# Attention with linear weights into a SwiGLU layer on one core: the first batch's loads, the order of the first weights, and the fourth batch's loads

## The chip, the cores and the metric

The kernel runs on one core of one Trainium2 chip. The metric is the device time of one execution in microseconds (us). A core has five engines that run side by side, each with its own queue of instructions that it takes in order: PE (TensorE, matmuls; its weight loads, PEld, overlap them), DVE (VectorE), ACT (ScalarE), POOL (GpSimd) and SP (SyncE, here for transfers alone). Transfers are issued from the queues of SP, ACT and POOL and run on 16 DMA engines that all of them share. An instruction waits for semaphores of others; what stands behind it on its engine waits with it.

## The reference

Eight batches of eight heads, 576 positions of 64 features. With `c`, `s` the cosine and sine of `pi/2 * pos/576`, every row of q and k becomes `[relu(x)*c, relu(x)*s]` (128 features). Attention is linear: K'V first, then Q' times that, over a denominator.

```
kv  = einsum('bhsf,bhsd->bhfd', k_p, v);  z = sum(k_p, axis=2)
num = einsum('bhsf,bhfd->bhsd', q_p, kv)
den = einsum('bhsf,bhf->bhs', q_p, z)[..., None] + 1e-06
x   = (num / den), heads side by side, reshaped to (4608, 512)
xn  = x / sqrt(mean(x*x) + 1e-6) * rms_g
out = (silu(xn @ w_gate) * (xn @ w_val)) @ w_out      # 512 -> 1536 -> 512
```

## The kernel before

**Tiles of the attention.** A batch's 576 positions are spread over 128 partitions: a pair of partitions shares 9 positions, 4 for one and 5 for the other (lines 83 to 87), so a batch is four tiles of 128 positions, j or t = 0 to 3, and a fifth that is half full (J). For this reason each load (`load`, line 92) is two DMAs, one for the even and one for the odd partitions, with 4 or 5 positions (1024 or 1280 B of float32) in a row; `cuts` splits the positions, so that a part can arrive earlier, in shorter rows. In the first batch k comes whole, q in positions 0 to 1 and 2 to 4, and v likewise, all issued from SP (lines 120 to 126). Batches 1 and 2 are loaded from POOL; from batch 3 on k and q come from ACT and v from POOL. v lands as bf16 from batch 1 on, which only POOL's transfers can do; the weights too.

**Steps of a tile.** `k_feat`, `q_feat` (lines 235, 247) make one half (cosine or sine, c = 0 or 1) of a feature tile on DVE or ACT; `v_cast` (238) copies v beside a column of ones. `kv_mm` (262) adds eight matmuls of tile j to K'V of all heads, in a PSUM tile of two banks (`att_tile`, two buffers), and `kv_evict` (275) copies it to SBUF on ACT. A q tile is turned either by a DMA from SP (`q_turn`, 281) or by eight PE transposes and a copy (`q_turn_pe`, `q_evict`, 290 to 305; PSUM from `ps_gv`, three buffers that the gate and value matmuls use as well). `num_mm` (309) makes numerator and denominator, `divide` (335, DVE) the quotient, `sumsq` (353) the sum of squares on ACT and its power -1/2, `rs`, on POOL, `norm` (364, DVE) the normed row; `x_turn_pe` and `x_evict` (380 to 392), or a DMA, turn it into columns of a block.

**Blocks of the feed-forward.** Nine blocks of 512 rows (the ninth is made of the half tiles J) run through `step(blk, nn)`, nn = 0 to 11 (line 626): gate matmuls to `gps`, value matmuls to `vps`, ACT's silu (`sil`), DVE's product `hT`, and from block 2 on four of the 48 output matmuls of the block before (`out_mm`, 438), which after each twelfth has ACT copy the result (`osb`) and SP store it (two DMAs). The first blocks take their columns in parts (`PARTS`), so that they can begin with fewer tiles. The 48 output matmuls of block 0 run in `lead()` (663), ahead of block 1, and fill the gaps of batch 1's preparation there.

**The order around it.** Everything is kept in the order of the program. Inside `step` the attention work of later batches is placed by a list: `at(g, kind, f, ...)` puts a call into step g (counted over all blocks) at one of the kinds `sp, act0, dve0, mid, act1, dve1, pe`, which `step` runs at fixed places:

```
run(g, "sp"); run(g, "act0"); run(g, "dve0")
gps matmuls; run(g, "mid"); vps matmuls
sil; run(g, "act1"); run(g, "dve1"); hT; out_mm x4 (from block 2 on); run(g, "pe")
```

**Weights.** `load_gv(c)` (209) issues two DMAs from POOL, a third of gate and of value weights; `load_wo(c)` a third of the output weights. Before, POOL first copies one element of the first cast v tile (`pool_after`, line 738), which holds its queue until then; thirds 0 and 1 follow, third 2 after `x_evict((0, 0))` (line 761), and at step 3 `more_loads` (152) issues the output weights and batches 1 and 2. At most eight of POOL's transfers are under way: each waits until the eighth before it has landed.

**Block 0's start** (lines 722 to 763) is written out: 34 warm-up matmuls on a tile of ones, features of k and of two q tiles, two turned q tiles, v casts with `kv_mm`, `num_mm`, and so on until the first normed tile is in place.

## Time and profile before

| what | value |
|---|---|
| median of 3 runs (lowest, highest) | 336.58 us (336.23, 337.99) |
| the profiled execution | 337.09 us, span on the core 334.9 us |
| busy in the span: PE, PEld | 318.3 us (95%), 213.4 us (64%) |
| busy in the span: DVE, ACT, POOL | 190.2 us (57%), 169.2 us (51%), 47.9 us (14%) |
| mean granted TensorE clock | 0.999 |
| moved by DMA | 50.63 MB, mean 151 GB/s |

The profile is of one execution. Its page lists busy times, forty slices, the DMA queues, the chain of waits that ended last, and groups of instructions; the trace behind it answers for single stretches: the timeline (start, duration, engine, line, operation; in square brackets the engine's idle time before it and what ended that), the waits by engine, the table by stretches (busy time of each engine, the granted clock, the share of the 16 DMA engines and GB/s, counted as written), and the DMA queues (q1 is issued by SP, q10 by ACT, q0 by POOL). A line such as L414 is a line of the kernel; L414 and L401 are gate and value matmuls, L446 output matmuls, L718 warm-up matmuls, L267 K'V, L316 the numerators, L294 and L384 the transposes on PE. A busy PE counts warm-up matmuls too, so its share says nothing of useful work at the start.

Some marks of the start, from the timeline and the transfers' times to landing (us from the span's start):

| event | us |
|---|---|
| k landed (two halves) | 5.3 and 7.2 |
| first q_turn_pe | 10.51 |
| first weight DMA issued | 12.51 |
| v's last cut landed, gb landed, q's last cut landed | 12.9, 13.6, 15.5 |
| kv_evict, first num_mm | 14.66, 15.30 |
| first gps matmul, first vps matmul | 20.30, 22.06 |
| lead() begins on PE | 44.1 |
| block 1, step 12, begins on PE | 60.1 |

### The profile page before, as it was taken

The numbers are of one execution on the slowest core, as the hardware profiler recorded it, in microseconds if no ns is written. First come the engines' busy times: TensorE is split into PE (matmuls) and PEld (weight loads), VectorE is DVE, ScalarE is ACT, GpSimd is POOL, SyncE is SP. The second block draws the span as 40 slices with busy tenths as digits, with TensorE's granted clock in tenths as the row PEclk, the third lists the DMA queues.
The fourth block names the chain that finished last, engine by engine and source line by source line (L and its number), as shares of the span: only waits on it lengthen the run. The fifth ranks groups of instructions, "written<-read, shape, count | busy, mean of one in ns | idle before, by whom it ended". The sixth has DMA issues, their size and how long they took to land.

```text
span 334.9 us, 7537 instructions
## 1 busy us (share of the span) xinstructions
PE 318.3 (95%) x3009; PEld 213.4 (64%) x3045; DVE 190.2 (57%) x394; ACT 169.2 (51%) x320; POOL 47.9 (14%) x91
## 2 busy tenths in 40 slices
PE   6679999998999999999999999999999999999995
PEld 4568856996887788778877744454444444444443
DVE  5676476776866575588857686665652422222300
ACT  3764377775875447486646474644433322233221
POOL 3446361300012120031103001000100000000000
PEclk9999999999999999999999999999999999999999
DMA  7999999893239989999969994253123021000012
GB/s 219 273 205 184 229 296 348 228 234 95 65 96 197 239 202 169 283 272 202 167 120 237 291 165 110 65 142 80 47 65 94 32 65 46 34 33 31 31 63 96
DMA packets 82147, 50.63 MB, mean 151 GB/s; under 512 B 49056, under 2 KB 76464, under 8 KB 82112
## 3 DMA queue, kind: packets, MB, share of 16 engines
q1 hardware_dynamic: 58032, 24.65, 33.8%
q0 software_dynamic: 13360, 13.57, 22.7%
q10 hardware_dynamic: 10720, 11.93, 12.2%
q8 instruction: 24, 0.39, 0.5%
q14 instruction: 11, 0.09, 0.1%
HBM read 38.01 MB, written 9.44 MB: 142 GB/s over the span
## 4 chain that ended last, share of the span: by engine, by line
PE 80%; DMA 7%; DVE 5%; ACT 4%; issue 2%; ACTq 1%; POOL 1%; SPq 0%; DVEq 0%
PE acc L446 25%; PE gps L401 12%; PE vps L401 12%; PE gps L414 12%; PE vps L414 12%; DMA rqT<-qp 3%; PE att L316 3%; DMA wv<-in_moe_w_val_dram 3%; PE att L267 2%; DMA kbuf<-in_k_dram 2%; DVE kp L231 1%; ACT kp L229 1%; PE qtp L294 1%; DVE xn L366 1%; PE acc L781 1%
## 5 line engine op out<-in xcount | busy, mean ns | idle before, releaser
L653 DVE TENSOR_TENSOR hT<-vps,sil 128x512 bf16<-128x512 f32 x108 | 74.5, 690 | 98.9 <-PE vps L401 59.6
L647 ACT ACTIVATE sil<-gps 128x512 bf16<-128x512 f32 x108 | 64.5, 597 | 109.6 <-PE gps L401 61.9
L446 PE MATMUL acc<-wo,hT 128*128 128x512 bf16 x395 | 101.8, 379 | 1.9 <-ACT osb L452 0.6
L446 PEld LDWEIGHTS <-hT 128*128 128x128 bf16 x420 | 40.0, 98 | 40.5 <-issue 0.9
L414 PE MATMUL gps<-xnT,wg 128*128 128x128 bf16 (+1 forms) x704 | 62.7, 239 | 0.7 <-ACT xnT L392 0.7
L414 PE MATMUL vps<-xnT,wv 128*128 128x128 bf16 (+1 forms) x704 | 62.8, 239 | 0.5 <-DMA wv<-in_moe_w_val_dram 0.5
L414 PEld LDWEIGHTS <-wg 128*128 128x128 bf16 x704 | 50.2, 98 | 6.8 <-DMA wg<-in_moe_w_gate_dram 0.6
L414 PEld LDWEIGHTS <-wv 128*128 128x128 bf16 x704 | 51.3, 98 | 3.8 <-DMA wv<-in_moe_w_val_dram 0.7
L361 POOL TENSOR_TENSOR rs<-ss,mhalf 128x1 f32<-128x1 f32 x36 | 20.1, 559 | 200.1 <-ACT sq L356 200.0
L401 PE MATMUL gps<-xnT,wg 128*128 128x512 bf16 x139 | 36.7, 379 | 0.4
L401 PE MATMUL vps<-xnT,wv 128*128 128x512 bf16 x141 | 36.5, 379 | 0.1
L452 ACT COPY osb<-acc 128x512 f32<-128x512 f32 x35 | 20.4, 583 | 26.4 <-PE acc L446 21.8
L401 PEld LDWEIGHTS <-wv 128*128 128x128 bf16 x192 | 18.8, 98 | 22.7
L366 DVE SCALAR_TENSOR_TENSOR xn<-x,rs,gb 128x512 bf16<-128x512 f32 x36 | 26.9, 748 | 8.8 <-POOL rs L361 8.8
L401 PEld LDWEIGHTS <-wg 128*128 128x128 bf16 x192 | 18.0, 98 | 20.1
L345 DVE TENSOR_TENSOR x<-att,rec 128x512 f32<-128x512 f32 x36 | 24.9, 691 | 1.2
L231 DVE TENSOR_SCALAR kp<-kbuf,trig 128x512 bf16<-128x512 f32 x50 | 22.8, 489 | 3.1 <-DMA kbuf<-in_k_dram 2.7
L231 DVE TENSOR_SCALAR qp<-qbuf,trig 128x512 bf16<-128x512 f32 x52 | 23.9, 485 | 0.4 <-DMA qbuf<-in_q_dram 0.4
L356 ACT ACTIVATE sq<-x 128x513 f32<-128x513 f32 x36 | 22.6, 626 | 2.9 <-DVE x L345 2.5
L229 ACT ACTIVATE kp<-kbuf,trig 128x512 bf16<-128x512 f32 x30 | 20.6, 712 | 3.4 <-DMA kbuf<-in_k_dram 3.4
L316 PEld LDWEIGHTS <-rqT 128*128 128x128 bf16 x320 | 14.3, 98 | 9.1 <-issue 1.1
L229 ACT ACTIVATE qp<-qbuf,trig 128x512 bf16<-128x512 f32 x28 | 19.6, 714 | 0.4 <-DMA qbuf<-in_q_dram 0.4
(63 smaller groups left out, 193.2 us busy)
## 6 DMA issues: line engine op xcount, KB each, us to landing
out_dram<-osb SPq DMA_DIRECT2D x70, 128.0 KB, 2.6
kbuf<-in_k_dram ACTq DMA_DIRECT2D x5, 640.0 KB, 6.1
qbuf<-in_q_dram ACTq DMA_DIRECT2D x5, 640.0 KB, 8.2
kbuf<-in_k_dram ACTq DMA_DIRECT2D x5, 512.0 KB, 4.8
qbuf<-in_q_dram ACTq DMA_DIRECT2D x5, 512.0 KB, 6.5
vbuf<-in_v_dram POOLq DMA_DIRECT2D x7, 320.0 KB, 9.4
vbuf<-in_v_dram POOLq DMA_DIRECT2D x7, 256.0 KB, 6.7
wg<-in_moe_w_gate_dram POOLq DMA_DIRECT2D x3, 512.0 KB, 10.1
```

Of the source, the lines that this page charges most:

```text
L229: K(nc.scalar.activation(out=dst, in_=src, func=AF.Relu, scale=scale))
L231: K(nc.vector.tensor_scalar(out=dst, in0=src, scalar1=scale, scalar2=0.0, op0=ALU.mult, op1=ALU.max,))
L316: K(nc.tensor.matmul(nums[key][:, h // Z, (h % Z) * E : (h % Z) * E + D + 1], lhsT=rqT[a, t][:, h, :], rhs=kvm[a % NK][:, h, 0 : D + 1], s ...
L345: K(nc.vector.tensor_tensor(out=x[:, 0:DM].rearrange("p (z s d) -> p z s d", z=2, d=D), in0=a[:, :, :, 0:D], in1=r.unsqueeze(3).to_broadca ...
L356: K(nc.scalar.activation(out=sq[:, :], in_=xs[key][:, :], func=AF.Square, scale=1.0 / math.sqrt(DM), accum_out=ss[:, :],))
L366: K(nc.vector.scalar_tensor_tensor(out=xn[:, :], in0=xs.pop(key)[:, 0:DM], scalar=rss.pop(key)[:, :], in1=gb[:, :], op0=ALU.mult, op1=ALU. ...
L401: K(nc.tensor.matmul(ps[:, :], lhsT=w[:, dt, nn * P : (nn + 1) * P], rhs=xnT[blk][:, dt, :], start=(dt == 0), stop=(dt == NDT - 1),))
L414: K(nc.tensor.matmul(ps[:, i * cn : (i + 1) * cn], lhsT=w[:, dt, (n0 + i) * P : (n0 + i + 1) * P], rhs=xnT[blk][:, dt, c0 : c0 + cn], star ...
L446: K(nc.tensor.matmul(acc[blk][:, :], lhsT=hT[blk][:, nn, jt * P : (jt + 1) * P], rhs=wo[:, nn, :], start=(nn == 0), stop=(nn == NNT - 1),))
L452: K(nc.scalar.copy(out=osb[:, :], in_=acc[blk][:, :]))
L647: K(nc.scalar.activation(out=sil[:, :], in_=gp[:, :], func=AF.Silu))
L653: K(nc.vector.tensor_tensor(out=dst, in0=a, in1=c, op=ALU.mult))
```

## The change

- **First batch's loads.** v comes in whole rows (no cuts). Of k the half with five positions is issued by ACT, and behind it, from ACT too, the weights of the norm (`gb`), which is now ahead of q; the rest stays on SP: half of k, q 0 to 1, v, q 2 to 4.
- **Features.** The first q tile's halves are made before the last k half of DVE (2, 1) and of ACT (4, 1).
- **Weights.** POOL's gate is now the first half of the first q tile (DVE); behind it all six gate and value DMAs and two of the three output weights are issued in one row. The third follows at step 0, with batch 1's k; q and v of batch 1 at step 2, batch 2 at step 3.
- **First K'V.** All v casts are placed ahead of the matmuls, tiles 1 and 3 on ACT; the order of tiles is 0, 1, 2, 4, 3; five warm-up matmuls go. K'V lies in two tiles of one bank each, from `ps_gv`, and ACT copies the first, DVE the second.
- **First normed tile.** `x_evict((0, 0))` is DVE's; `norm((0, 1))` stands before `divide((0, 2))`.
- **Kinds.** A kind `act2` behind `act1` takes ACT's features, casts and loads; in each third step from block 2 on it runs after the output matmuls. `q_turn` moves from `dve1` to `pe`.
- **Batch 1 and 2 in block 1.** q tile J of batch 1 goes from step 13 to 12, the first q tile of batch 2 from 14 to 13.
- **Fourth batch (b = 3).** k and v are issued in `lead()`, ahead of block 1, q at step 15, all from POOL.

```diff
@@ -89,14 +89,15 @@
 
 
 
+
     def load(t, src, b, odd_five=False, cuts=(0, NC5)):
-        if b == 0:
-            eng = nc.sync
-        else:
-            eng = nc.scalar if b > 2 and src is not v else nc.gpsimd
         for lo, hi in zip(cuts[:-1], cuts[1:]):
             for par, t0, jn in lanes(odd_five):
                 z = min(hi, jn)
+                if b == 0:
+                    eng = nc.scalar if src is k and jn == NC5 else nc.sync
+                else:
+                    eng = nc.scalar if b > 3 and src is not v else nc.gpsimd
                 K(eng.dma_start(
                     out=t[par:P:2, :, lo * D : z * D],
                     in_=src[b, :, :, :].rearrange("h (i j) d -> i h (j d)", j=NT)[
@@ -118,11 +119,11 @@
     clear_fifth(v0, nc.vector)
     gb = consts.tile([P, DM], FP32, name="gb")
     load_k(0)
-    load_q(0, (0, 2))
-    load_v(0, (0, 2, NC5))
-    K(nc.sync.dma_start(
+    K(nc.scalar.dma_start(
         out=gb[:, :], in_=moe_rms_g.rearrange("(o d) -> o d", o=1).to_broadcast([P, DM])
     ))
+    load_q(0, (0, 2))
+    load_v(0)
     load_q(0, (2, NC5))
 
 
@@ -259,13 +260,22 @@
     def att_heads(a):
         return a[:, :, 0 : Z * E].rearrange("p z (s w) -> p z s w", w=E)
 
+    def kv_banks(b):
+
+        t = kvp[b]
+        return t if b == 0 else [t[:, z, :] for z in range(2)]
+
     def kv_mm(b, j, first, last):
         if first:
-            kvp[b] = att_tile()
+            kvp[b] = (
+                [ps_gv.tile([P, TB], FP32, name="kv0", tag="gv") for _ in range(2)]
+                if b == 0 else att_tile()
+            )
+        banks = kv_banks(b)
         for h in range(H):
 
             K(nc.tensor.matmul(
-                kvp[b][:, h // Z, (h % Z) * E : (h % Z) * E + D + 1],
+                banks[h // Z][:, (h % Z) * E : (h % Z) * E + D + 1],
                 lhsT=kp[j][:, h, :, :].rearrange("p c d -> p (c d)"),
                 rhs=vx[j][:, h, 0 : D + 1],
                 start=(first and h % Z == 0),
@@ -274,9 +284,17 @@
 
     def kv_evict(b):
         dst = kvm[b % NK][:, :, :].rearrange("p (z s) w -> p z s w", z=2)
-        K(nc.scalar.copy(
-            out=dst[:, :, :, 0 : D + 1], in_=att_heads(kvp.pop(b))[:, :, :, 0 : D + 1]
-        ))
+        if b == 0:
+            for z, t in enumerate(kvp.pop(b)):
+                src = t[:, 0 : Z * E].rearrange("p (s w) -> p s w", w=E)[:, :, 0 : D + 1]
+                if z == 0:
+                    K(nc.scalar.copy(out=dst[:, z, :, 0 : D + 1], in_=src))
+                else:
+                    K(nc.vector.tensor_copy(out=dst[:, z, :, 0 : D + 1], in_=src))
+        else:
+            K(nc.scalar.copy(
+                out=dst[:, :, :, 0 : D + 1], in_=att_heads(kvp.pop(b))[:, :, :, 0 : D + 1]
+            ))
 
     def q_turn(b, t):
         tt = rqtp.tile([P, H, P], BF16, name="rqT", tag="rqT")
@@ -453,7 +471,7 @@
             out_store(blk, jt, osb)
 
 
-    KINDS = ("sp", "act0", "dve0", "mid", "act1", "dve1", "pe")
+    KINDS = ("sp", "act0", "dve0", "mid", "act1", "act2", "dve1", "pe")
     NS = (B + 1) * NNT
     plan = {(g, w): [] for g in range(NS) for w in KINDS}
 
@@ -475,18 +493,18 @@
     def feat_at(g, f, b, j, act):
         for c in range(2):
             on_act = c == 1 and act
-            at(g, "act1" if on_act else "dve0" if f == k_feat else "dve1", f, b, j, c, on_act)
+            at(g, "act2" if on_act else "dve0" if f == k_feat else "dve1", f, b, j, c, on_act)
 
     def q_at(g, b, t, act=False):
         feat_at(g, q_feat, b, t, act)
         if t < J:
-            at(g, "dve1", q_turn, b, t)
+            at(g, "pe", q_turn, b, t)
 
     def k_at(g, b, j, act=False):
         feat_at(g, k_feat, b, j, act)
 
     def v_at(g, b, j):
-        at(g, "act1", v_cast, b, j, True)
+        at(g, "act2", v_cast, b, j, True)
 
     def kv_at(g, b):
         for j in range(NC5):
@@ -513,18 +531,12 @@
         at(3, "dve1", q_feat, 0, J, c)
 
 
-    def more_loads():
-        for c in range(NG):
-            load_wo(c)
-        load_k(1)
-        load_q(1, (0, 2))
-        load_v(1)
-        load_q(1, (2, NC5))
-        load_k(2)
-        load_q(2)
-        load_v(2)
-
-    at(3, "pe", more_loads)
+    at(0, "pe", load_wo, 2)
+    at(0, "pe", load_k, 1)
+    for f, *a in ((load_q, 1, (0, 2)), (load_v, 1), (load_q, 1, (2, NC5))):
+        at(2, "pe", f, *a)
+    for f in (load_k, load_q, load_v):
+        at(3, "pe", f, 2)
 
     def pe_tile_at(g, key, xblk, col, gx):
 
@@ -537,9 +549,9 @@
 
     def q2_at(g, b, t):
         for c in range(2):
-            at(g, "act1" if c else "dve1", q_feat, b, t, c, c == 1)
+            at(g, "act2" if c else "dve1", q_feat, b, t, c, c == 1)
         if t < J:
-            at(g, "dve1", q_turn, b, t)
+            at(g, "pe", q_turn, b, t)
 
 
     at(12, "dve0", divide, (1, 2))
@@ -551,28 +563,27 @@
         at(12 + t, "dve0", norm, (1, t))
         at(12 + t, "pe", x_turn_pe, (1, t))
         at(13 + t, "act1", x_evict, (1, t), 1, t)
-    q2_at(13, 1, J)
+    q2_at(12, 1, J)
 
 
     for g, j, c in ((14, 2, 1), (15, 1, 0), (16, 0, 0), (16, 2, 0), (17, 3, 0), (17, 4, 0),
                     (17, 3, 1), (17, 4, 1)):
-        at(g, "act1" if c else "dve1", k_feat, 2, j, c, c == 1)
+        at(g, "act2" if c else "dve1", k_feat, 2, j, c, c == 1)
     for j in range(NC5):
-        at(18, "act1" if j > 2 else "dve1", v_cast, 2, j, j > 2)
+        at(18, "act2" if j > 2 else "dve1", v_cast, 2, j, j > 2)
     kv_at(18, 2)
-    for t, g in enumerate((14, 19, 20, 21, 23)):
+    pe_tile_at(19, (2, 0), 2, 0, 21)
+    for t, g in enumerate((13, 19, 20, 21, 23)):
         q2_at(g, 2, t)
-    pe_tile_at(19, (2, 0), 2, 0, 21)
     pe_tile_at(22, (2, 1), 2, 1, 24)
     pe_tile_at(24, (2, 2), 2, 2, 26)
     pe_tile_at(25, (2, 3), 2, 3, 27)
 
 
-    for o, f in ((12, load_k), (13, load_v), (15, load_q)):
-        at(o, "act1", f, 3)
+    at(15, "pe", load_q, 3)
     for j in range(NC5):
         for c in range(2):
-            at(22 + j, "act1" if c else "dve1", k_feat, 3, j, c, c == 1)
+            at(22 + j, "act2" if c else "dve1", k_feat, 3, j, c, c == 1)
         at(22 + j, "dve1", v_cast, 3, j)
     kv_at(27, 3)
     for t, g in enumerate((24, 25, 27, 28, 29)):
@@ -591,7 +602,7 @@
             (g1, g1 + 2, g1 + 4, g1 + 6),
         ))
         for o, f in zip(loads, (load_k, load_v, load_q)):
-            at(o, "act1", f, b)
+            at(o, "act2", f, b)
         for j, o in enumerate(preps):
             k_at(o, b, j, j > 1)
             v_at(o, b, j)
@@ -646,6 +657,9 @@
         sil = silp.tile([P, TB], BF16, name="sil", tag="sil")
         K(nc.scalar.activation(out=sil[:, :], in_=gp[:, :], func=AF.Silu))
         run(g, "act1")
+        ends = blk > 1 and nn % 3 == 2
+        if not ends:
+            run(g, "act2")
         run(g, "dve1")
         a, c = vp[:, :], sil[:, :]
         if blk in PARTS:
@@ -654,6 +668,8 @@
         if blk > 1:
             for i in range(4 * nn, 4 * nn + 4):
                 out_mm(blk - 1, i)
+        if ends:
+            run(g, "act2")
         run(g, "pe")
 
     def outs(lo, hi):
@@ -698,6 +714,8 @@
         norm((1, 0))
         outs(36, 40)
         q_turn_pe(1, 3)
+        load_k(3)
+        load_v(3)
         x_turn_pe((1, 0))
         x_evict((1, 0), 1, 0, dve=True)
         q_evict(1, 3)
@@ -722,24 +740,25 @@
     warm_up(34)
     for j in range(NC5):
         for c in range(2):
+            if (j, c) in ((2, 1), (NC5 - 1, 1)):
+                q_feat(0, 0, int(j > 2), act=(j > 2))
             k_feat(0, j, c, act=(j > 2))
-    for t in range(2):
-        for c in range(2):
-            q_feat(0, t, c, act=(c == 1))
+    for c in range(2):
+        q_feat(0, 1, c, act=(c == 1))
+    pool_after(qps[0, 0][0:1, 0, 0, 0:1])
+    for c in range(NG):
+        load_gv(c)
+    for c in range(2):
+        load_wo(c)
     q_turn_pe(0, 0)
     q_evict(0, 0, dve=True)
     q_turn_pe(0, 1)
     q_evict(0, 1)
     warm_up(8)
     for j in range(NC5):
-        v_cast(0, j, act=(j == 3))
-        kv_mm(0, j, j == 0, j == NC5 - 1)
-        if j == 0:
-            pool_after(vx[0][0:1, 0, 0:1])
-            load_gv(0)
-            load_gv(1)
-        if j == 1:
-            warm_up(5)
+        v_cast(0, j, act=(j % 2 == 1))
+    for j in (0, 1, 2, 4, 3):
+        kv_mm(0, j, j == 0, j == 3)
     kv_evict(0)
     num_mm((0, 0))
     num_mm((0, 1))
@@ -757,10 +776,9 @@
     num_mm((0, 2))
     q_feat(0, 3, 0, act=True)
     x_turn_pe((0, 0))
-    x_evict((0, 0), 0, 0)
-    load_gv(2)
+    x_evict((0, 0), 0, 0, dve=True)
+    norm((0, 1))
     divide((0, 2))
-    norm((0, 1))
 
 
     for blk in range(B + 1):
```

## The prediction

> **What bounds it now.** I read the busy shares first: PE is busy 95% of the 334.9 us span, DVE 57%, ACT 51%. So only time in which PE stands still can be won. The list of PE's waits says where that is.
>
> ```profile
> PE qtp L294 <- ACT qp L229: 2.6, 2, 2.1
> PE xps L384 <- DVE xn L366: 1.3, 3, 0.7
> PE att L316 <- DMA rqT<-qp: 0.8, 1, 0.8
> ...
> PE vps L414 <- DMA wv<-in_moe_w_val_dram: 0.5, 1, 0.5
> ```
>
> Next the table by stretches: in 0 to 22 us PE is idle 7.8 us (and its warm-up matmuls count as busy), afterwards only here:
>
> ```profile
> 44.00:60.00 16.00, 15.14 (x150) 8.75 (x151) 11.63 (x27) 12.39 (x22) 5.26 (x8) 1.00 1.16 310
> ...
> 72.00:88.00 16.00, 14.47 (x187) 12.83 (x187) 10.93 (x26) 11.53 (x23) 1.11 (x2) 1.00 0.52 120
> ```
>
> The second figure is the stretch, the third PE's busy time: 0.86 and 1.53 us are lost. In 30 to 44 us PE is busy 14.00 of 14.00. Third, the chain of waits, which for the start reads:
>
> ```profile
> 1.56 5.61 DMA kbuf<-in_k_dram
> ...
> 12.26 0.31 POOL probe L223
> 12.57 0.85 POOL wg L211
> 13.42 8.60 DMA wv<-in_moe_w_val_dram
> 22.02 0.05 issue
> 22.06 1.07 PE vps L414 x16
> ```
>
> k lands at 7.2; the weights wait for the first cast of v at 12.2, and wv's first third lands at 22.0, where PE needs it. But a second chain is as late: v's last cut lands at 12.9, kv_evict ends at 15.25, num_mm starts at 15.30, and through divide, sumsq, rs, norm, x_turn_pe and ACT's x_evict the first gps starts at 20.30 (timeline). Both must move. Last, PE's timeline around the two late stalls:
>
> ```profile
> 77.42 0.43 PE L316 MATMUL att<-kvm,rqT 128*128 128x65 bf16 x8 [0.80 <-DMA rqT<-qp]
> ...
> 82.06 0.40 PE L384 MATMUL xps<-ident_b,xn 128*128 128x128 bf16 x4 [0.72 <-DVE xn L366]
> ```
>
> **The start, DMA side.** v in whole lanes has rows of 1024 and 1280 B instead of 512 and 768 B. While k (rows of those sizes) flows, 4 to 6 us, the core moves 394 GB/s; while v's small rows flow, 8 to 10 us, 291. v's 1.18 MB by landings takes 3.9 us (three cuts 0.9 apart and 1.2 for the last); at 394 it is 3.0: -0.9. gb moves ahead of q: its 0.7 us (v's last landing 12.9, gb's 13.6) now lies before q and v: +0.7. v's last landing: 12.9 - 0.9 + 0.7 = 12.7, and all of q, k, v, gb ends 0.9 earlier.
>
> k over two queues: its 640 KB half leaves SP (0.73 us of issue) and is issued by ACT at 1.45 (after kbuf's memset) or, if the table load holds ACT's queue, at 2.02; no row here tells. Either way it now shares the engines with q instead of going ahead of it: half of q's 512 B rows, some 0.5 us, can come first. I take k at 7.7 (7.0 to 8.0) and q's first cut at 8.9 + 0.7 = 9.6.
>
> **The start, engines.** Started one behind the other, k's features take 0.62 us each on ACT (four in 2.56) and 0.41 on DVE (six in 2.47). ACT now runs three of them, 7.8 to 9.65, then the q feature to 10.3; so q_turn_pe(0, 0) starts at 10.4 (10.51 before). The gate is DVE's first q feature: five k features at 0.41 and q end at 10.3, probe 0.3, first weight issue at 10.6 against 12.51. The rest waits for v: casts on DVE to 13.95; on ACT, behind q_evict(0, 1), to 14.4; the last kv_mm (0.25 for eight) to 14.7 against 14.62. The five warm-up matmuls taken out filled that same wait and cost nothing. The eviction in two tiles: the last copies have 128x256 at 0.37 on ACT and 0.42 on DVE against 0.59 for the whole: num_mm at 15.2, -0.1. x_evict(0, 0) on DVE, 0.42 for 0.58: -0.16. First gps: 20.05.
>
> POOL now issues eight weight DMAs in one row, and rs(0, 0) queues behind them, wanted at 17.6. The rows run from 0.69 (DVE quiet) to 0.91 (DVE casting); eight are 5.5 to 7.3 us, so POOL is free between 16.1 and 17.9: 0 to +0.3. I take 0.8, done at 17.0: nothing. The Trainium skill, "SBUF — State Buffer", section "SBUF: two separate sides", speaks against the row of issues: while DVE runs some copies, GpSimd is locked out and cannot write descriptors. By that rule DVE's some 2 us of casts from 10.6 on would be added to 5.5: free at 18.1, +0.5; the 0.91 beside casts agrees in sign, not in that size.
>
> wv's first third no longer decides: the plain loads end 0.9 earlier, and the slow start of the weights' stream (some 80 GB/s between 14.5 and 15.5 against 206 later, worth 0.6 us) now lies beside them; 22.0 - 0.9 - 0.6 = 20.5, and vps wants it at 21.2 (gps 0.9 and x_turn_pe 0.25 later). So the first vps goes from 22.06 to 21.2. Much is given back: norm((0, 1)) now stands before divide((0, 2)) on DVE. DVE: x_evict to 20.0, norm to 20.75, divide 1.1, q feature 0.5, x_evict 0.4; sumsq and rs (1.4 after divide) let norm((0, 2)) end at 24.05, and its x_turn_pe holds the second vps at 24.35 against 24.69. **Start: -0.3.** Bounds: -1.3 (k not late, DVE's order free) and +1.7 (first rival).
>
> **The lead.** The nine weight DMAs and k(1) now follow without the break that the profile has at 30 to 32 us (119 GB/s instead of 206). k(1), landed at 44.9, comes some 2 us earlier. ACT, free from 44.0, waited 0.98 for it; its four k features, osb copy and q feature then end before PE asks at 48.1, and DVE's q feature (to 48.2) remains: PE's 0.56 there becomes some 0.1. **-0.5** (0 to -0.86, the stretch's whole idle).
>
> **Steps 12 to 22.** k and q of batch 3 leave ACT's queue: 1.6 us of issue between sumsq and sil at 61.55 to 63.2, and 1.2 at 67. q_feat(2, 0) moves from step 14 to 13 and q_feat(1, J) to 12; DVE's 0.72 of idle before hT at 62.12 covers the latter. rqT(2, 0) is then issued near 65 less what was won, before q(3) (now step 15, POOL). At 67.03 it was issued with q(3) and v(3) and took 10.34 us; the median transpose takes 3.9. Even at 10 us it lands before 76.6, when PE asks: -0.8. In step 20 sumsq now precedes the q feature (act2), 0.61 less in the chain to the late xps: -0.65. **-1.45** (0 to -1.7). If k(3) on POOL were slow, nothing waits: its features are due at 84, it is issued near 57, behind rs(1, 0) and rs(1, 1).
>
> **The rest.** q_turn now queues on SP behind a step's out_store: up to one step (2.6 us) later; num_mm comes three steps later, and 3.9 us of transpose fit. ACT's features behind osb in each third step may save PE's 0.6 of waits for osb: **-0.1** (+0.6 to -0.6).
>
> **Sum.** -0.3 - 0.5 - 1.45 - 0.1 = -2.35. The profiled execution took 337.09 us, 2.2 of it around its span; 334.7 for it. The median shown, 336.58, is 0.5 lower: 334.2.
>
> **Rivals.**
>
> *The rest of q is late.* q's last two cuts (1024 rows) are sent last, when the weights' packets now flow. If the rings alternate, some 560 rows left at 12.6 pair with weight packets (201 per us, 80 ns of 16 engines, against 34): 4.0 us, landing 17.6 instead of 15.5. sumsq((0, 0)) stands behind these q features on ACT: +1.7 at the start, 336.2. The rule is in "DMA: Bandwidth & Descriptors" of the Trainium skill, section "Queues, rings and completion order": each engine goes round its rings by packet. Against it is the stretch 14.5 to 15.0, when both had packets: what was in the ring first went first, 88 rows to 39.
>
> ```profile
> q0 software_dynamic: 39, 0.04, 113.9%
> q1 hardware_dynamic: 88, 0.06, 39.6%
> ```
>
> *The rest of q is starved: slower.* In 67 to 70 us it was the other way:
>
> ```profile
> q0 software_dynamic: 779, 0.42, 110.6%
> q10 hardware_dynamic: 138, 0.16, 14.4%
> ```
>
> v(3) had the engines, and the q DMA issued there took 9.4 us. If two of the weights' DMAs (2.55 us each) go in front of q's rest, it lands near 19.8, start +4: 338.5; with all eight 354. It is slower by over 0.5% if q's rest lands after 19.5.
>
> *The transpose's wait is only moved* (another transfer or DVE at step 21): the -1.45 falls away, 335.7. For it: DVE is 80% busy in 60 to 72.
>
> *The start gives nothing back* (k early, DVE's order harmless): -1.3, 333.2. For it, PE waits 2.1 us on ACT's q there; against it, v's landing.
>
> **How the numbers follow.** Forecast 0.45 (333.2 to 335.4); q's rest late 0.18; starved 0.10; wait moved 0.12; start in full 0.15. 0.5%, about what can be told from no change, is 1.7 us: faster is below 334.9. From the forecast some 0.38, all of the last 0.15 and 0.05 from the others: 0.58 faster; slower 0.12 (the starved case and unknowns); 0.30 between. The range runs from 332.3 to 336.8 and leaves out mostly the starved case.
>
> **What would show it.** Right: wv landed before the first vps; first gps near 20; no wait for rqT or 0.1 at the (2, 0) tiles; ACT's idle before the k(1) features gone. Wrong: ACT idle before the q features of tile 2 until after 16 us; rs(0, 0) behind weight issues; qtp later than 10.5; a new PE wait in 88 to 200.

## The result, and the profile after

The changed kernel is slower. Its median is 339.44 us (20 runs, 336.57 to 350.03) against 336.74 (20 runs, 336.18 to 340.21) for the kernel before on the same chip; the ratio of the compared runs is 1.0054, with an interval of 1.0028 to 1.008. The ratio leaves out runs more than 1.5% above a kernel's fastest, of which some of the kernels below have many, so the tables give the median of all runs, as its difference to the kernel before that ran beside it (here +2.70 us; the median before lies between 336.14 and 336.74 everywhere), and this ratio with its 95% interval next to it.

The profiled execution took 340.75 us, its span 338.6 (before 337.09 and 334.9). Line numbers moved: gate and value matmuls are now L432 and L419, output matmuls L464, warm-up L736, K'V and numerators L277 and L334, the transposes on PE L312 and L402, `q_turn` L301. PE's waits (total, times, longest):

```profile
PE qtp L312 <- ACT qp L230: 4.4, 2, 3.8
...
PE att L334 <- DMA rqT<-qp: 2.7, 1, 2.7
PE xps L402 <- DVE xn L384: 1.0, 3, 0.4
```

The wait for ACT's first q features grew from 2.6 to 4.4 us, one of 2.7 us for a turned q tile is new (the 0.8 us before were at another tile, near 77), and the wait for xn fell. The table by stretches (stretch, length, busy time of PE, PEld, DVE, ACT, POOL; granted clock, DMA share, GB/s):

```profile
12.00:22.00 10.00, 7.88 (x110) 6.42 (x111) 6.21 (x15) 6.88 (x13) 7.63 (x11) 0.83 1.20 233
22.00:30.00 8.00, 7.49 (x107) 7.26 (x105) 5.39 (x13) 2.72 (x5) 2.78 (x5) 0.79 1.24 206
...
44.00:60.00 16.00, 15.86 (x159) 10.38 (x159) 10.84 (x26) 11.20 (x20) 4.42 (x7) 1.00 1.03 280
...
72.00:88.00 16.00, 15.61 (x213) 14.27 (x211) 11.22 (x27) 11.93 (x22) 0.56 (x1) 1.00 0.39 109
150.00:160.00 10.00, 7.21 (x103) 5.78 (x103) 6.48 (x15) 4.98 (x12) 1.11 (x2) 1.00 1.26 254
```

The last of these stretches read, in the kernel before:

```profile
150.00:160.00 10.00, 9.90 (x146) 8.22 (x146) 8.77 (x19) 6.66 (x14) 1.37 (x3) 1.00 1.34 195
```

Both stretches that were to gain did: PE is busy 15.86 us in 44 to 60 (15.14 before) and 15.61 in 72 to 88 (14.47). The loss is in 0 to 30, where the granted clock also fell to 0.83 and 0.79 (1.00 before), and in 150 to 160. The chain of waits for the start (start, duration, what):

```profile
2.23 8.91 DMA qbuf<-in_q_dram
11.22 0.72 ACT qp L230
...
13.23 1.03 PE qtp L312 x8
...
22.65 1.51 PE gps L432 x16
24.16 0.43 PE xps L402 x4
24.59 1.71 PE vps L432 x16
```

It no longer begins with k but with q's first cut, which landed at 9.97 and 11.14 (8.08 and 8.98 before). The weights are not late: wv's first third landed at 21.89, the first vps came at 24.59 behind its own tile. Where the 3.7 us of span went, as the lag behind the kernel before at the same instruction:

| mark | before | after | lag |
|---|---|---|---|
| first q_turn_pe | 10.51 | 12.00 | +1.5 |
| first gps | 20.30 | 22.65 | +2.35 |
| `lead()` begins on PE | 44.10 | 47.44 | +3.3 |
| first out_mm of block 2 | 88.04 | 89.52 | +1.5 |
| end of the span | 334.9 | 338.6 | +3.7 |

The changed kernel is late by 3.3 when `lead()` begins, has won 1.8 of it back by block 2, and loses 2.7 again at 150 (some 0.5 is won in between). The timeline of PE at the late xps that the prediction showed with 0.72 us, and at the new wait:

```profile
83.54 0.40 PE L402 MATMUL xps<-ident_b,xn 128*128 128x128 bf16 x4 [0.39 <-DVE xn L384]
```
```profile
153.69 0.63 PE L334 MATMUL att<-kvm,rqT 128*128 128x65 bf16 x15 [2.73 <-DMA rqT<-qp]
```

SP's queue ahead of it, first in the kernel before, then after (start, time for the group, line, operation, how many):

```profile
125.23 6.22 SPq L283 DMA_TRANSPOSE rqT<-qp  x2
131.57 1.98 SPq L436 DMA_DIRECT2D out_dram<-osb  x2
133.67 9.76 SPq L283 DMA_TRANSPOSE rqT<-qp  x4
```
```profile
126.74 2.35 SPq L301 DMA_TRANSPOSE rqT<-qp  x1
131.30 1.11 SPq L454 DMA_DIRECT2D out_dram<-osb  x2
133.05 15.97 SPq L301 DMA_TRANSPOSE rqT<-qp  x5
```

One transpose that stood ahead of the output store now stands behind it, and the fifth of the row, issued at 144.73, landed at 153.65.

### The profile page after: what moved, and what is told of

The parts are those of the page before. It is cut to its first block, busy times and chain, and to the rows that moved or that the text cites. A ratio compares the mean times of both kernels' runs of the same rounds, so it can differ in the third digit from the quotient of the medians.

```text
span 338.6 us, 7535 instructions
## 1 busy us (share of the span) xinstructions
PE 319.9 (94%) x3004; PEld 215.6 (64%) x3040; DVE 189.8 (56%) x395; ACT 168.5 (50%) x320; POOL 50.9 (15%) x95
## 4 chain that ended last, share of the span: by engine, by line
PE 87%; DMA 5%; DVE 3%; issue 1%; ACT 1%; SPq 0%; POOL 0%; DVEq 0%; ACTq 0%
PE acc L464 25%; PE gps L432 14%; PE vps L432 14%; PE gps L419 12%; PE vps L419 12%; PE att L334 3%; DMA rqT<-qp 3%; DMA qbuf<-in_q_dram 3%; PE att L277 3%; PE qtp L312 1%; PE xps L402 1%; DVE xn L384 1%; PE acc L799 1%; DVE x L363 1%; PE wps L736 1%
## 5 line engine op out<-in xcount | busy, mean ns | idle before, releaser
L464 PE MATMUL acc<-wo,hT 128*128 128x512 bf16 x395 | 101.7, 379 | 1.3
L464 PEld LDWEIGHTS <-hT 128*128 128x128 bf16 x420 | 40.0, 98 | 39.6
L432 PE MATMUL gps<-xnT,wg 128*128 128x128 bf16 (+1 forms) x704 | 63.2, 239 | 0.6 <-DVE xnT L408 0.5
L432 PE MATMUL vps<-xnT,wv 128*128 128x128 bf16 (+1 forms) x704 | 63.6, 241 | 0.0
L432 PEld LDWEIGHTS <-wg 128*128 128x128 bf16 x704 | 50.6, 98 | 6.7 <-issue 0.8
L432 PEld LDWEIGHTS <-wv 128*128 128x128 bf16 x704 | 52.1, 99 | 3.0
L419 PE MATMUL gps<-xnT,wg 128*128 128x512 bf16 x139 | 36.7, 379 | 0.4
L419 PE MATMUL vps<-xnT,wv 128*128 128x512 bf16 x141 | 36.5, 379 | 0.1
L419 PEld LDWEIGHTS <-wv 128*128 128x128 bf16 x192 | 18.8, 98 | 22.7
L419 PEld LDWEIGHTS <-wg 128*128 128x128 bf16 x192 | 18.0, 98 | 20.1
L334 PEld LDWEIGHTS <-rqT 128*128 128x128 bf16 x320 | 14.4, 98 | 11.3 <-DMA rqT<-qp 3.3
```

The costliest lines, as they stand in the source:

```text
L334: K(nc.tensor.matmul(nums[key][:, h // Z, (h % Z) * E : (h % Z) * E + D + 1], lhsT=rqT[a, t][:, h, :], rhs=kvm[a % NK][:, h, 0 : D + 1], s ...
L419: K(nc.tensor.matmul(ps[:, :], lhsT=w[:, dt, nn * P : (nn + 1) * P], rhs=xnT[blk][:, dt, :], start=(dt == 0), stop=(dt == NDT - 1),))
L432: K(nc.tensor.matmul(ps[:, i * cn : (i + 1) * cn], lhsT=w[:, dt, (n0 + i) * P : (n0 + i + 1) * P], rhs=xnT[blk][:, dt, c0 : c0 + cn], star ...
L464: K(nc.tensor.matmul(acc[blk][:, :], lhsT=hT[blk][:, nn, jt * P : (jt + 1) * P], rhs=wo[:, nn, :], start=(nn == 0), stop=(nn == NNT - 1),))
```

## The experiments

In the tables "vs before" is the median minus that of the kernel before that ran beside it, in us; "ratio" is that of the compared runs, with its interval.

### First set: the suspects of the profile, one at a time

**e1: gb behind v, on SP.**

```diff
-    K(nc.scalar.dma_start(out=gb ...))   # ahead of q
+    K(nc.sync.dma_start(out=gb ...))     # behind load_v(0)
```

> The changed kernel with gb alone moved back: issued by SP behind v, ahead of q's last cuts. Theory A (gb's 2048 B rows on ACT's ring take the engines from q's 512 B rows, so q's first cut lands at 11.1 instead of 9): q's first cut lands near 9.5, the first q_turn_pe starts near 10.4 instead of 12.0, the first gps near 21 instead of 22.65, and the time falls by 1.5 to 2.5 us. Rival (k's half on ACT's ring is what holds q up): q's first cut stays after 10.5 and the time falls by less than 0.7 us.

**e2: the kinds of q_turn and act2 undone.** Act2 then runs right behind act1 in every step; ACT's features still stand behind what act1 holds, which was not so in the kernel before.

```diff
-            at(g, "pe", q_turn, b, t)
+            at(g, "dve1", q_turn, b, t)
-        ends = blk > 1 and nn % 3 == 2
+        ends = False
```

> The changed kernel with q_turn back at dve1 and act2 always right behind act1 (the kinds as before). Theory B (a transpose that was ahead of step 38's output store now stands behind it on SP, so the last of five transposes lands at 153.65 and PE waits 2.73 us for it in step 45): that wait is gone, the last of these transposes lands before PE's step 45, and the time falls by 2 to 3 us. Rival (the transfers of batch 5 from ACT are what delays it): the wait stays over 1.5 us and the time moves by less than 1 us.

**e3: more warm-up matmuls** (34 to 64 at the start, 5 to 13 behind the third turned q tile, 2 and 4 around `x_turn_pe((0, 0))`), so that the clock stays up while PE waits for q.

```diff
-    warm_up(34)
+    warm_up(64)
...
-    warm_up(5)
+    warm_up(13)
...
+    warm_up(2)
     x_turn_pe((0, 0))
+    warm_up(4)
```

> The changed kernel with 30 more warm-up matmuls ahead of the first q_turn_pe and 14 more up to the first gps, so that PE is hardly idle before block 0. Theory C (PE's idle 3.8 us from 8.2 on let the granted clock fall to half in 12.7 to 16.2 and again in 23.0 to 26.4, where the first gps and vps took 1.51 and 1.71 us instead of 0.89): the granted clock stays at 1.00 from 6.4 us to the end, the first gps and vps take about 1.05 and 0.9 us, and the time falls by 1.0 to 2.0 us; the spread of the runs narrows to that of the kernel before. Rival (the fall of the clock lies beside waits for data and costs nothing): clock at 1.00, time within 0.5 us.

**e4: k and gb both on SP in the old order**, v still whole: e1's edit and

```diff
-                    eng = nc.scalar if src is k and jn == NC5 else nc.sync
+                    eng = nc.sync
```

> The changed kernel with k and gb of the first batch all on SP in the order of before (k, q 0 to 1, v, gb, q 2 to 4); v stays in whole lanes. Theory A: q's first cut lands near 9.0 as before and the first q_turn_pe starts near 10.4; against the run with gb alone moved back it is within 0.7 us. Rival (k on two queues costs as well): 1 us or more faster than that run. Against the changed kernel 2 to 3 us faster.

| kernel | median (lowest to highest) | vs before | ratio | first gps |
|---|---|---|---|---|
| e1 | 338.62 (334.34 to 348.77) | +2.48 | 1.0021 (0.9991 to 1.0051) | 20.40 |
| e2 | 337.45 (335.86 to 342.15) | +1.31 | 1.0040 (1.0019 to 1.0060) | 22.32 |
| e3 | 342.54 (338.29 to 353.13) | +6.40 | 1.0117 (1.0080 to 1.0155) | 20.98 |
| e4 | 339.56 (335.37 to 349.19) | +3.42 | 1.0021 (0.9995 to 1.0046) | 19.68 |

The start's cause is gb: with it behind v the first q_turn_pe came at 10.55 in place of 12.00. Whole loads from SP (e4) bring the first gps to 19.68, ahead of the kernel before. In e2 the wait of step 45 is gone, with a smaller gain than the 2 to 3 us expected. In e3 the granted clock is 1.00 in 0 to 22 us and the first gps 1.7 us earlier, of which 0.8 were there at the first q_turn_pe already. But a mended start bought little: by the medians nothing in e1, e3 or e4, by the ratios some 1.1 us in e1 and e4, and the runs spread over 14 us. e3's profile shows it given back at two transposes, at 150.3 and 154.8 us, so step 45's wait can be larger than in the changed kernel's own profile:

```profile
PE att L334 <- DMA rqT<-qp: 6.1, 2, 4.3
```

e1's shows a wait of 5.0 us ahead of the numerators of tile (2, 0), the first turned tile of batch 2, whose transpose took 14.1 us:

```profile
81.55 0.62 PE L334 MATMUL att<-kvm,rqT 128*128 128x65 bf16 x8 [4.98 <-issue]
```

So a third cause had to be found. The tile had landed at 79.31, though, and "issue" says that the profile names nothing that ended the last 2.2 us. e8 below has the same: the tile landed at 76.12, PE began at 78.01. Both times PE began 1.5 us behind the end of a 16 KB packet of the queue `q8 instruction`, which started at 78.98 and 75.34; in e10 below, where no transpose is slow, the packet in that place (the second behind 62 us) started at 69.37. So the same jam may have held up PE's instructions as well; that PE waited for them is not shown.

### Second set: both suspects undone, then one more part

**e5: e4's loads and e2's kinds together.**

> The change with its two suspects undone together: k and gb on SP in the old order (v stays whole), and q_turn at dve1 with the features of act2 always ahead of hT. Theory: the two causes are separate and add up, the kinds by 2.0 us (339.4 to 337.45 in the run that undid them alone) and the loads by 2 to 3 us (first gps 19.7 in place of 22.65): 334.5 to 335.5, ratio to before 0.994 to 0.998; no wait for rqT in step 45; first gps near 19.7. Rival: what is left of the late transpose of tile (2, 0), issued in the same half microsecond as batch 3's q from POOL, costs as much as the start wins: 336 to 337, ratio 0.999 to 1.003, with PE waiting for rqT at 76 to 82 us.

**e6: e5, and batch 3's loads as before the change.**

```diff
-        load_k(3); load_v(3)            # in lead(), POOL
-    at(15, "pe", load_q, 3)             # POOL
+    for o, f in ((12, load_k), (13, load_v), (15, load_q)):
+        at(o, "act1", f, 3)             # k and q from ACT, v from POOL
```

> The same kernel with batch 3's k and q loads issued by ACT and v's by POOL at steps 12, 13 and 15, as before the change. Theory: the early loads of k(3) and v(3) are what won the 1.1 us in 72 to 88 us, so this is 0.8 to 1.4 us slower than the kernel with them early: 335.5 to 336.5. Rival 1: rqT(2, 0) meets the q load of batch 3 either way, and the early loads win nothing: equal within 0.4 us. Rival 2: with the loads on ACT the transposes are spared: faster.

**e7: the kernel before with the kinds of the change alone.** The lists change `act1` to `act2` as in the diff of the change, and

```diff
-            at(g, "dve1", q_turn, b, t)
+            at(g, "pe", q_turn, b, t)
+        ends = blk > 1 and nn % 3 == 2      # act2 behind the output matmuls
```

> The kernel before with one part of the change alone: q_turn from dve1 to pe, the kind act2 behind act1, and act2 behind the output matmuls in each third step. Theory: this part by itself brings the wait of step 45 (the fifth of a row of transposes behind an out_store): PE waits 1 to 4 us for rqT near 150 us, 337.5 to 339.0, ratio 1.003 to 1.008. Rival: the wait needs the later start (the start and the queue of the transposes shift alike): 336.0 to 336.8 and no wait for rqT there.

**e8: e5 with q of batch 3 two steps later in the list.**

```diff
-    at(15, "pe", load_q, 3)
+    at(17, "pe", load_q, 3)
```

> The first kernel of this call (loads and kinds undone) with q of batch 3 issued at step 17 in place of 15, so that it no longer flows beside the transpose of tile (2, 0). Theory: that pair is what makes the runs of the changed kernel spread; here the spread of its runs falls to that of the kernel before (some 3 us between lowest and highest) and the median is 0.3 to 1.0 us below the first kernel's. Rival: the transpose is slow beside any other work or the spread has another source: same median within 0.3 us and the same spread.

| kernel | median (lowest to highest) | vs before | ratio | transpose of tile (2, 0), issue to landing |
|---|---|---|---|---|
| e5 | 338.40 (334.24 to 342.42) | +2.00 | 0.9998 (0.9969 to 1.0027) | 16.5 us |
| e6 | 334.57 (333.97 to 335.01) | -1.83 | 0.9950 (0.9937 to 0.9963) | 4.7 us |
| e7 | 335.19 (334.28 to 338.11) | -1.21 | 0.9985 (0.9960 to 1.0010) | 10.5 us |
| e8 | 340.64 (334.74 to 344.53) | +4.24 | 0.9991 (0.9963 to 1.0018) | 11.6 us |

e5's rival held by its ratio and its wait (the median is above the 337 it named), and so did e6's second rival: batch 3's early loads do not win, they cost 3.8 us by the medians and 1.6 by the ratios, and make the spread. e7's theory fell: the kinds alone do not make the kernel before slower (its median is lower, the interval of its ratio includes 1), and no wait of step 45 came of them. In e5 the queue of SP, that of POOL and PE's timeline read:

```profile
64.69 23.76 SPq L301 DMA_TRANSPOSE rqT<-qp  x4
```
```profile
64.63 1.44 POOL L101 DMA_DIRECT2D qbuf<-in_q_dram  x2
```
```profile
81.25 0.62 PE L334 MATMUL att<-kvm,rqT 128*128 128x65 bf16 x8 [5.26 <-DMA rqT<-qp]
```

q of batch 3 goes out with the transpose, and PE waits 5.26 us; the granted clock is 0.50 for the 3.4 us behind that wait. The two go together because both hang on ACT's sumsq, which ends at 64.05: behind it come a feature on ACT (0.71 us), then the transpose, and an rs on POOL (0.55 us), then the load. e8 did not part them: POOL does not follow PE's steps. It issues as soon as the work ahead in its queue is done (an rs that waits for ACT, here) and the buffer is free, and the load "of step 17" left at the same place:

```profile
64.48 1.43 POOL L101 DMA_DIRECT2D qbuf<-in_q_dram  x2
```

The DMA queues of e5 in 71 to 79 us (packets, MB, share of 16 engines; q1 are the transposes, q0 the load):

```profile
DMA packets 668, 0.47 MB, mean 59 GB/s; under 512 B 610, under 2 KB 610, under 8 KB 666
...
q1 hardware_dynamic: 605, 0.15, 67.2%
q0 software_dynamic: 61, 0.29, 40.8%
```

The engines count as fully busy and move 59 GB/s: a packet of 256 B of the transpose takes 0.672 x 8 us x 16 / 605 = 0.14 us, one of 4 to 5 KB of the load 0.86. This is the worst of the stretch: in 66 to 69 us the transpose got 99 packets through, of 0.05 us, beside 237 of POOL's queue of 0.20.

### Third set: that part alone, and with one DMA moved

**e9: the changed kernel, with only batch 3's loads put back** (e6's edit).

> The changed kernel as it is, with batch 3's loads alone put back (k and q from ACT, v from POOL, at steps 12, 13, 15). Theory: the early loads leave q of batch 3 to be issued by POOL in the same microsecond as the first transpose of batch 2, and the two hold each other up; with them back the spread falls below 5 us and the median to 336.8 to 338.3, that is 334.6 (loads, kinds and batch 3 undone) plus 2.2 for the late start and 0 to 1.5 for step 45. Rival: start and step 45 are the whole loss of the changed kernel: 339 or more, spread as wide as the changed kernel's 13 us.

**e10: e5 with q of batch 3 alone issued by ACT.**

```diff
-    at(15, "pe", load_q, 3)       # POOL
+    at(15, "act1", load_q, 3)     # ACT
```

> The kernel with loads and kinds undone (338.4 us, 334.2 to 342.4), and only q of batch 3 issued by ACT at step 15 as before; k and v of batch 3 stay early on POOL. Theory: the transpose meets POOL's q load; without it the transpose of tile (2, 0) lands within 6 us, and the time is that with all of batch 3 put back, 334.2 to 335.2, spread below 3 us. Rival: the early k and v of batch 3 themselves do it (v still flows when the transpose is issued): transpose 9 us or more, median above 336.5, spread above 5 us.

**e11: e4 with batch 3's loads put back**; the kinds stay as changed.

> k and gb on SP in the old order and batch 3's loads put back; the kinds stay as the change has them. Theory: the kinds alone cost or win little when nothing else is late (335.2 for them alone on the kernel before, 336.4 without): 334.0 to 335.5, rqT wait of step 45 at most 1 us. Rival: they cost 1 us or more here as they did in the changed kernel: 335.6 to 337.

**e12: the kernel before with batch 3's loads of the change alone** (e6's diff the other way round, on the kernel before).

> The kernel before with batch 3's loads of the change alone: k and v from POOL in front of block 1, q from POOL at step 15. Theory: this part by itself makes the runs spread (6 us or more between lowest and highest) and slower, median 337.5 to 340, with the transpose of tile (2, 0) landing after 9 us or more and PE waiting for it by 2 us or more in many runs. Rival: it needs the earlier issue of the transpose that the other parts bring (64.7 in place of 67.0): 335.5 to 336.8 with the spread of the kernel before.

| kernel | median (lowest to highest) | vs before | ratio | transpose of tile (2, 0) |
|---|---|---|---|---|
| e9 | 336.76 (335.65 to 338.81) | +0.53 | 1.0019 (1.0003 to 1.0035) | 4.5 us |
| e10 | 334.60 (333.96 to 336.60) | -1.63 | 0.9956 (0.9939 to 0.9973) | 4.4 us |
| e11 | 333.92 (333.73 to 334.05) | -2.31 | 0.9932 (0.9915 to 0.9948) | 4.4 us |
| e12 | 335.91 (334.79 to 339.75) | -0.32 | 1.0002 (0.9978 to 1.0027) | 7.8 us |

e9 went nearly as its theory had it: 336.76 us, the runs within 3.2 us. One DMA pair, q of batch 3, is worth 3.6 us by the medians (e10 against e5, +2.00 to -1.63) and 1.4 by the ratios. Early k and v of batch 3 win nothing. e12's theory fell: there POOL issued q at 65.47 and the transpose followed at 67.23, the load went ahead and no wait came of it. The harm needs the meeting that the other parts brought about. e11, the change without its new queue and order for k and gb and without batch 3's early loads, beats both kernels.

### Fourth set: the meeting or the queue, and the two DMAs of the start

**e13: e11, with k over two queues as in the change** (gb stays on SP): e4's line for k goes back to `nc.scalar if src is k and jn == NC5 else nc.sync`.

> Kinds as the change has them, batch 3 put back, gb on SP behind v, and k still over two queues (half from ACT). Beside it stands the same with k whole on SP (333.92 us; first q_turn_pe 9.8, first gps 19.65) and with gb on ACT as well (336.76; 11.66, 22.42). Theory: gb's wide rows are what delays q; k over two queues costs the 0.7 us by which the first q_turn_pe came later with it (10.5 against 9.8): 334.3 to 335.0, first gps 20.2 to 20.6. Rival: the two share the loss by halves, since any DMA on ACT's ring takes the engines from q: 335.1 to 336, first gps 21.

**e14: e5 with q of batch 3 from ACT at step 13**, right behind the feature that the transpose waits for.

```diff
-    at(15, "pe", load_q, 3)       # POOL
+    at(13, "act2", load_q, 3)     # ACT, behind q_feat(2, 0, 1)
```

> The kernel with loads and kinds undone and k and v of batch 3 early on POOL, and q of batch 3 issued by ACT at step 13, right behind the feature that the first transpose of batch 2 waits for, so that both are issued within a microsecond. With q from POOL in that place it took 338.4 us (334.2 to 342.4) and the transpose 16.5 us; with q from ACT at step 15 334.6 and 4.4 us. Theory 1: it is the meeting in time, from whichever queue: transpose 9 us or more, median above 336.5, spread above 5 us. Theory 2: it is POOL's queue: transpose within 7 us, median 334.2 to 335.5, spread below 3 us.

**e15: e5 with q of batch 3 from POOL, held until a feature of step 16.**

```diff
-    at(15, "pe", load_q, 3)
+    at(16, "pe", lambda: (pool_after(kp[2][0:1, 0, 0, 0:1]), load_q(3)))
```

> The same, with q of batch 3 from POOL, but held there by a copy of one element of a feature of step 16, near 70 us, when the transpose of tile (2, 0) has landed. Theory 1 (the meeting in time): transpose within 6 us, median 334.0 to 335.3, spread below 3 us. Theory 2 (POOL's queue makes any transpose slow, the next at 77 us too, or q comes late for its features at step 24): median above 336.

**e16: the changed kernel with kinds and batch 3's loads put back.**

> The changed kernel with kinds and batch 3's loads put back; k over two queues and gb on ACT stay. With the kinds kept it took 336.76 us. Theory: the kinds win some 0.7 us where no transpose is slow (333.92 against 334.57 with the loads plain), so 337.2 to 337.8 here; their loss of 2.0 us beside the early loads of batch 3 was those transposes'. Rival: with the late start the kinds cost time by themselves through step 45: 335.0 to 336.4.

| kernel | median (lowest to highest) | vs before | ratio | transpose of tile (2, 0) |
|---|---|---|---|---|
| e13 | 335.29 (334.31 to 337.01) | -1.23 | 0.9954 (0.9930 to 0.9978) | 4.6 us |
| e14 | 334.69 (334.29 to 337.53) | -1.83 | 0.9949 (0.9930 to 0.9967) | 9.5 us |
| e15 | 334.39 (333.99 to 336.94) | -2.13 | 0.9955 (0.9932 to 0.9979) | 4.4 us |
| e16 | 337.27 (336.41 to 338.00) | +0.75 | 1.0017 (1.0000 to 1.0035) | 6.3 us |

e13's time is in its rival's range, but its start is not late: first gps at 19.78, so the cause that the rival names is not in its profile. e15 settles it for the meeting: the same load from the same queue, issued at 68.85 when the transpose has landed, and the loss is gone. Its queues in 66 to 69 us (the transpose, with 144 packets of v beside it) and in 70 to 74 (the load alone):

```profile
q1 hardware_dynamic: 1057, 0.28, 66.6%
q0 software_dynamic: 144, 0.08, 19.5%
```
```profile
q0 software_dynamic: 265, 1.14, 91.0%
```

That is 0.030 us for a packet of the transpose and 0.22 for one of the load, a fifth and a quarter of what they took when they met. e14 lies between its theories: the transpose took 9.5 us, as the meeting says, but it landed before PE asked, and the time is that of no loss. The two halves of the load were issued from ACT at 63.32 and 64.17, ahead of the transpose at 64.6. So the queue may have a share in how bad a meeting is. In the kernel before and in e7 the load came from ACT in the same 0.03 us as the transpose, which took 10.3 and 10.5 us, and PE waited 0.80 and 0.95; from POOL, within 0.1 us, the transpose took 8.3 (e2), 10.0 (e3), 10.8 (e4), 11.6 (e8), 14.1 (e1) and 16.5 us (e5). e16 went as its theory had it.

### Fifth set: what was left of the start

**e17: e13 with the kinds put back too.**

> k over two queues (half from ACT), gb on SP behind v, batch 3's loads put back, and the kinds put back too. With the kinds of the change this took 1.23 us less than the kernel before; with k whole on SP as well 2.31 us less; with k whole on SP and the old kinds 1.83 us less. In the profile of the first the start was not later (first gps 19.8), but PE waited 1.75 us for rqT in step 45, where the old kinds show no wait. Theory: k over two queues costs in its start, in executions that the profile did not show: 0.6 to 1.1 us less than the kernel before. Rival: it costs nothing at the start and the 1.1 us were step 45's: 1.6 to 2.1 us less than the kernel before.

**e18: e11 again, on another chip.**

> The fastest version so far (k and gb on SP in the old order, batch 3's loads put back, all else as the change has it) on the chip of this call: 2.0 to 2.6 us less than the kernel before if its five runs told its time, spread below 1.5 us; 1.0 to 1.8 us less, with some runs 1 us or more above the lowest, if step 45's wait falls on it in some executions too.

| kernel | median (lowest to highest) | vs before | ratio |
|---|---|---|---|
| e17 | 334.88 (334.20 to 336.27) | -1.70 | 0.9949 (0.9929 to 0.9970) |
| e18 | 334.00 (333.83 to 342.57) | -2.58 | 0.9939 (0.9919 to 0.9958) |

e17's rival held: k over two queues costs 0.13 us (e6 against it, -1.83 to -1.70), too little to tell from nothing, so most of the 1.1 us that e13 lost against e11 is put down to step 45, where e13's profile has the wait of the changed kernel, 1.75 us. Why that wait falls on more executions of e13 than of e11 stays open. e18 confirms the median of e11, but two of its twelve runs took 336.0 and 336.3 and one 342.6. The profiled one (336.26) waits for rqT by 1.8 us in two waits, 0.3 in step 45 and 1.5 at 161.9, so such waits are in e11's kernel too, in few executions. What the run of 342.6 met is not known; no profile shows it.

### The sum of the parts

| put back, one after the other | vs before | what this won | ratio |
|---|---|---|---|
| nothing: the changed kernel | +2.70 | | 1.0054 (1.0028 to 1.0080) |
| batch 3's loads (e9) | +0.53 | 2.17 | 1.0019 (1.0003 to 1.0035) |
| and the kinds (e16) | +0.75 | -0.22 | 1.0017 (1.0000 to 1.0035) |
| and gb (e17) | -1.70 | 2.45 | 0.9949 (0.9929 to 0.9970) |
| and k on SP (e6) | -1.83 | 0.13 | 0.9950 (0.9937 to 0.9963) |
| the last, with the kinds as changed (e11) | -2.31 | 0.48 | 0.9932 (0.9915 to 0.9948) |

Each row is against the kernel before that ran beside it. By the medians gb and batch 3's loads cost 4.6 us, by the ratios 3.5; what is left of the change wins 2.3. The changed kernel's own profile shows the first of the two and step 45; the slow transpose of tile (2, 0) is not in it (it landed in 5.8 us). That other executions of it have that transpose is concluded from medians and spread (336.57 to 350.03, in e9 335.65 to 338.81) and from the profiles of e1, e5 and e8. It is not shown in a profile of the changed kernel itself.

## Why the prediction was wrong, step by step

**The start, DMA side, failed: "gb moves ahead of q: its 0.7 us ... now lies before q and v".** This term was too small. It was added as time on one road: so many bytes, so much later. q's first cut was forecast to be complete at 9.6; its halves landed at 9.97 and 11.14, the second 2.2 us later than with gb behind v (8.89 in e1, all else the same). Other runs agree: in the five profiles with gb ahead of q it was complete at 10.24 to 11.14, in all others at 8.55 to 8.98. gb and half of k stand in ACT's ring, q in SP's, and the engines took one packet from each in turn. The DMA queues of the changed kernel in 5.0 to 6.5 us, and those of e11 in 6.5 to 8.0 with q alone:

```profile
q10 hardware_dynamic: 312, 0.40, 74.5%
q1 hardware_dynamic: 301, 0.15, 35.4%
```
```profile
q1 hardware_dynamic: 860, 0.45, 120.9%
```

312 packets of k against 301 of q: one for one, so q's 512 B rows got a third of the engines' time and went at 200 in a us in place of 570. The Trainium skill has this in "DMA: Bandwidth & Descriptors", section "Queues, rings and completion order": each engine goes round its rings by packet. The trace agrees, one for one; the prediction used the rule only for q's rest. But turns with k cost nothing in the end: e1 has them too (305 packets of k, 293 of q in the same 1.5 us), and there q's first cut landed as in the kernel before (8.98). The loss came behind k, with gb's rows of 2048 B. The queues of the changed kernel in 7 to 8 us:

```profile
q10 hardware_dynamic: 98, 0.18, 84.9%
q1 hardware_dynamic: 109, 0.05, 21.8%
```

The core moved 234 GB/s there, and a packet of gb took 0.15 us in the mean, where it took 0.095 in the kernel before, in SP's ring. Its 128 packets are 1.2 us of 16 engines in place of 0.76. That is half of the 2.2 us; why gb's packets were slower, and what makes up the rest, no view shows. The first q_turn_pe came at 12.00 for 10.4, and PE, idle from 8.24 to 12.0, lost its clock as well. With gb behind v the rest of the term stands: in e11 v's last cut landed at 12.12, where the forecast without gb's 0.7 is 12.0, and the first gps is at 19.65, where the forecast said 20.05.

**"Steps 12 to 22": the gain was nearly right, one of its reasons was not, and the step after it failed.** From block 1's first gps to the first out_mm of block 2 PE took 27.97 us before, 26.67 after and 26.78 in e11: 1.30 and 1.20 won for 1.45 forecast: the 0.8 of rqT in full, half of the late xps (0.72 to 0.39). That k and q of batch 3 leave ACT's queue was not needed for it: e6 has those loads back on ACT, and took 26.75. The gain at the late xps goes with act2: in e7, with the kinds alone, no wait of xps for xn is over 0.3. The 0.8 of rqT does not (e7 waits 0.95 there); the q features a step earlier and the earlier start are left for it, and were not run apart. But "rqT(2, 0) is then issued near 65 less what was won, before q(3) (now step 15, POOL) ... Even at 10 us it lands before 76.6" took POOL to issue at step 15. POOL issued q(3) as soon as the rs ahead of it was done, within 0.1 us of the transpose in e5, and together they take not 10 us but up to 16.5. The bound of 0 on the side of a loss was one slow transpose of the kernel before taken as the worst there is.

**The lead was right.** From its first out_mm to block 1's first gps PE took 15.97 us before, 15.41 after and 15.40 in e11: 0.56 and 0.57 won for 0.5.

**The rest, priced at -0.1:** by medians the kinds won more from e6 to e11 (-0.48) and in e7 (-1.21) and lost 1.4 in the changed kernel (e2); none of the three is clear of the intervals. "3.9 us of transpose fit" was wrong for single executions, and the local rows said so: the six transposes that the kernel before issued from 125 to 141 us took 6.2 to 9.0 us to land. The issue of the row of five behind the store takes 11.1 us in e11 and 15.97 in the changed kernel; e11 has no wait there, the changed kernel 2.7 us, and e3 one of 4.3.

**POOL's row of weights** was priced at nothing, and rightly: eight issues ran from 12.10 to 18.41, and rs(0, 0) at 20.29 waited for ACT's sumsq. The rule of the Trainium skill's "SBUF — State Buffer", section "SBUF: two separate sides", by which DVE's casts would lengthen that row by 2 us, shows in no row at that size: the eight took 6.3 us, between the quiet 5.5 and the 7.3 of issues beside casts, and the two beside v's casts (14.60 to 15.88) 0.86 us each, those around them 0.75.

**The rivals.** q's rest was neither late nor starved (landed at 15.27 and 16.30). "The transpose's wait is only moved" came nearest, but it had the wait come back as it was, and it came back larger. No rival had gb. The chance of slower was 0.12, and the range ended at 336.8.

e11 with -2.31 us is close to the sum forecast for the whole change, -2.35, but in part by chance, for that sum had gb's 0.7 in its start. The terms for the parts that stayed were about right; gb was priced at a third of what it cost q, and q of batch 3 from POOL at nothing.

## What to carry to other kernels

A load moved to another queue does not queue up behind the first: the two take turns by packet, and the narrow rows can lose more than the other load's own time (2.2 us for gb's 0.76 here). Keep a load that nobody waits for off a second ring until the transfer that everything waits for is through; half of k, which was needed as early, shared the engines with q at no loss. An issue that is placed in a step of the program, but on an engine that does not keep to those steps, goes when its queue and buffer let it. Look for what leaves in the same microsecond, and if that is a DMA transpose, hold the load back (a copy of one element on POOL did it) or issue it from a queue that is in step. Where single runs of a kernel spread more than those of its neighbour, read several profiles before trusting one.

## What the runs showed of the hardware that was not expected

- A DMA transpose and a plain load of 4 to 5 KB packets from POOL, issued together, can hold each other up: in 71 to 79 us of e5 both ran at a quarter to a fifth of the speed they have in e15 (0.14 for 0.030 us, 0.86 for 0.22 us a packet), the engines counted busy, 59 GB/s moved. What the packets wait for no view shows; it stays open. With the load from ACT, in packets of 1024 and 1280 B and issued just ahead, the transpose took 9.5 us (e14), where it takes 4.4 with no q load beside it (e10, e15).
- The clock: PE stood idle 3.8 us at the start, and the trace then has two stretches of 3.41 us at half the clock, from 12.84 and from 23.08 us. 3.41 us at half make a mean of 0.83 over 12 to 22 and 0.79 over 22 to 30, the two values of the table. The Trainium skill's "TensorE: Matmul & The Clock Gate", section "Part 1: The HAM clock gate (the "warmup" mystery)", gives a free-running window of that length after which an idle PE is halved; the trace agrees in the length, but PE had been busy for 0.62 of the 3.41 us ahead of the first stretch and for 1.73 of those ahead of the second, so here an idle PE is not the whole condition. The first gps took 1.51 us, 1.05 in the kernel before. e1's wait, from 76.57 to 81.55, brought 6.83 us at half the clock, from 79.37 on.
